# A fixed list of operations for the attention, and its 32 x 32 inverses by blocks of 16

## The chip, the core and the metric

The kernel runs on one core of a Trainium2 chip. The metric is the device time of one execution in microseconds (us). The engines are named as in the profile: PE (TensorE, with PEld for its weight loads), DVE (VectorE), ACT (ScalarE), POOL (GpSimd), SP (SyncE). SP and POOL here mostly issue DMAs.

## The reference

The program has two parts. The first is a recurrent attention with a state of 40 x 40 for each of 4 x 8 pairs of batch and head, over 768 steps of time:

```python
for t in range(S):
    ...
    y[:, :, t] = np.einsum('bhd,bhde->bhe', rt, state)
    Sa = np.einsum('bhde,bhe->bhd', state, at)
    state_decay = state * wt[:, :, None, :] - np.einsum('bhd,bhe->bhde', Sa, bt)
    state = state_decay + np.einsum('bhd,bhe->bhde', vt, kt)
```

The second is an MLP on the 3072 rows of 320 that come out: `h = x @ w_in` (320 x 2048), `g = h * tanh(softplus(h))`, `g @ w_out` (2048 x 320). Everything is float32; the MLP's weights arrive as float64.

## The kernel before

The time axis is cut into 12 chunks of 64 steps. Inside a chunk, the recurrence becomes matrix products, with one small triangular matrix per head to be inverted; from chunk to chunk, only the state is passed on. Heads are packed in two halves `be` and two pairs of partitions `al`, so most tiles have 128 partitions.

- **Preparation**, `pre_a(c, be)` (L126), 24 times. SP loads `wa` and `bk` (two buffers each); DVE makes running products of the decay by two scans (L147, L157) and scales `a` and `bk` (L152, L170); ACT spreads `a` into `ad` (L155); PE multiplies `ad` and `bk` (L186) in three groups; ACT and DVE move the result out of PSUM into `GP` (what is to be inverted) and `HA` (L188 to L193); PE transposes `bk` (L202). POOL stores `P` to DRAM. `E`, the second scan's result, lies in the half of `wa` that held `a`.
- **Inverse**, `pre_inv(n)` (L205) and `post_inv(n)` (L223), six times, each for two chunks. A chunk's 64 x 64 triangle is two diagonal 32 x 32 triangles and a square. DVE turns the triangles round (L209) so that the 128 x 32 of them lie along partitions and free rows, inverts all at once by a loop over rows, i = 1 to 30, of a multiply (L214) and an add (L216), and turns them back into `TT` (L218, and for one half `T1`, L220). PE makes the square's part by two rounds of 32 x 32 products (L232, L241); ACT lays the three pieces into `bdT` (L249 to L251); PE multiplies `HA` by it (L258) into `KT` (L260).
- **Step**, `step(c)` (L349), twelve times, with two groups `g`. POOL loads `VS`, `UVT`, `bdr` (one buffer each; L267 to L271). In each group: `step_a`, state into `VS` (L277), products with `KT` (L284), into `UVT` (L286); `step_b`, products of `UVT` and `bdr` (L314), masked into `UVQ` by DVE (L316); `step_u` and `step_d`, transposes of `UVT` and of the state (L293, L304); `step_c`, the outputs and the state's change in one PSUM tile (L334, L339), the state updated by DVE (L342, L346), the output copied to `yev` by ACT (L343) and stored by POOL (L370).
- **MLP weights**: each piece is loaded as float64 pairs (`cv_d`, L453), turned into float32 by ACT and DVE (L459 to L463) and split into a high and a low part (L494, L495). `early` does the first quarter of `w_in` at the start, `first` the other three, `second` three eighths of `w_out`, `third`, inside the MLP, the rest. All conversion buffers ahead of the MLP are single.
- **MLP**, `run` (L550): twelve blocks of 256 rows and four quarters `q`, 32 matmuls of L583 and 24 of L603 to L605 each, with Mish on ACT.

The order of the instructions on each engine comes from a scheduler outside the source. It works on single instructions, by priority; the source raises or lowers the priority of parts with `at(tc, key)` and a table `OFF` of offsets, and lays out the rough order: preparations of pair 0, inverse 0, preparations of pair 1, then for each pair the string `ORDER = '0aiA1'`: step 0 of the pair, preparations two pairs on, the inverse one pair on, weights, step 1. So matmuls of different parts can stand mixed in PE's queue. PSUM is cut into four pools of two banks.

Of the kernel before, what the change touches and what calls it, by code (L numbers as in the profile page):

```python
# [7 lines left out]
F32 = mybir.dt.float32  # L8
F32R = mybir.dt.float32r
AF = mybir.ActivationFunctionType  # L10
ALU = mybir.AluOpType
# [6 lines left out]
NA = 2  # L18
NWA = 2
NKT = 4  # L20
NXL = 1
NTT = 1
NYEV = 1
NX2 = 1
NGP = 2
NG = 2
NQ = 2
QS = "SGGG"
NU = 2
NBR = 1  # L30
NAD = 2
NTMP = 1
NP = 2
NSTN = 1
LA = 2
ORDER = '0aiA1'

OFF = {'I': 80, 'T1': 80, 'P00': -40, 'P10': 80, 'P11': 40, 'b0': 15, 'c0': 600, 'u0': -15, 'u1': 250, 'd0': 250,
       'd1': 150, 'W': 600, 'V': 400, 'E': 150, 'I0': 600, 'I1': -15, 'I2': 15, 'I3': 150, 'I4': 80, 'p4': 15,
       'I5': -150, 'J5': 600, 's0': 150, 's2': -15, 's3': 80, 's4': 250, 's6': -15, 's7': -40, 's8': 150, 's10': -150}  # L40
SORD = 'a0 b0 u0 d0 a1 b1 u1 d1 c0 c1'


def at(tc, k):
    return tc.high_priority(offset=OFF[k]) if OFF.get(k) else nullcontext()
# [33 lines left out]
def attention(ctx, tc, I, yD, pD, nch, M):  # L79
# [4 lines left out]
    ps_u = pool("ps_u", NU, space=PSUM)  # L84
    ps_q = pool("ps_q", NQ, space=PSUM)
    ps_a = pool("ps_a", NA, ictx, "right", space=PSUM)
    M.early_pools(pctx)
    ps_g = pool("ps_g", NG, pctx, "right", space=PSUM)
    cs = pool("cs", 1)
    wk = pool("wk", 2)  # L90
    ci = pool("ci", 1, ictx)
    iw = pool("iw", 2, ictx)
    cp = pool("cp", 1, pctx, "right")
    pw = pool("pw", 2, pctx, "right")
# [6 lines left out]
    wab = [cp.tile([128, 1040], F32, name=f"wa{i}") for i in range(NWA)]  # L101
    bkb = [cp.tile([128, 8, 168], F32, name=f"bk{i}") for i in range(NWA)]
    adb = [cp.tile([128, 8, 2, 2, 32], F32, name=f"ad{i}") for i in range(NAD)] * (2 // NAD)
    d1 = cp.tile([128, 584], F32, name="d1")
    bdT = [ci.tile([128, 8, 2, 64], F32, name=f"bdT{i}") for i in range(2)]
# [5 lines left out]
    for t in [d1] + [x.rearrange("p s k a t -> p (s k a t)") for x in adb[:NAD]]:  # L111
        A.copy(t, z.broadcast_to(t.shape))
    for t in bdT:
        G.memset(t, 0.0)
    VS = [cs.tile([128, 2, 344], F32, name=f"VS{be}") for be in range(2)]
    UVT = cs.tile([128, 8, 256], F32, name="UVT")
    UVQ = [cs.tile([128, 16, 104], F32, name=f"UVQ{be}") for be in range(2)]
    bdr = [cs.tile([128, 2, 8, 2, 64], F32, name=f"bdr{i}") for i in range(NBR)] * (2 // NBR)
    ST = [cs.tile([128, 8, 64], F32, name=f"ST{g}") for g in range(2)]
    for t in VS + [UVT] + bdr[:NBR] + ST:  # L120
        G.memset(t, 0.0)
# [536 lines left out]
```

## Time and profile before

| | us |
|---|---|
| median of 3 runs | 844.03 |
| lowest, highest | 843.01, 845.59 |
| span of the profiled execution | 843.5 |
| PE busy in the span | 748.6 |
| DVE busy in the span | 462.0 |
| ACT busy in the span | 429.0 |
| POOL busy in the span | 103.3 |
| mean granted TensorE clock | 0.939 |

The profile is of one execution; its span goes from the first instruction to the last. A row of the page's groups has the line, engine and operation, output and inputs by name, shapes, count, then busy time in us and the mean of one in ns, then the engine's idle time just before, and who ended it. A row of a timeline has start and length in us. Matmul ends are modelled, about 0.2 us after the work of the last one. A row of stages has, after the stage's bounds and length, the busy time of PE, PEld, DVE, ACT and POOL with counts, the granted clock, the share of the DMA engines and the DMA rate. A row of waits has the waiting engine and line, the releaser, the total in us, the number of waits and the longest. A row of one line's instructions has the least, median and greatest duration in ns and the first and last start.

### The profile page before, as it was taken

How to read it: one execution, taken by the hardware profiler on the slowest of the kernel's cores; microseconds unless marked ns; L12 is line 12 of the kernel's file. 1: busy time of each engine (PE TensorE's matmuls, PEld its weight loads, DVE VectorE, ACT ScalarE, POOL GpSimd, SP SyncE). 2: the span in 40 equal slices, each digit the busy share in tenths (PEclk: the TensorE clock that was granted, in tenths of full speed). 3: DMA queues.
4: the chain of work that ended last, by engine and by line, in shares of the span. 5: the costliest groups of instructions: out<-in, count | busy, mean ns of one | idle time of the engine just before them, and what ended most of it. 6: DMA issues, size and time to landing. Idle time of an engine off the chain costs nothing.

```text
span 843.5 us, 18796 instructions
## 1 busy us (share of the span) xinstructions
PE 748.6 (89%) x7816; PEld 695.6 (82%) x7816; DVE 462.0 (55%) x975; ACT 429.0 (51%) x937; POOL 103.3 (12%) x182
## 2 busy tenths in 40 slices
PE   2645898998989889889799899999999999999998
PEld 2534697887868778778768799999999999999998
DVE  6789879739899658788924639221222222122110
ACT  4533647774586866566738546333333333333331
POOL 8100012113122023221101200000000000000000
PEclk9855689899999999899959999999999999999999
DMA  6422223323423233323425734211120111100000
GB/s 177 134 71 64 74 63 73 90 67 105 129 81 80 66 88 103 82 67 96 123 66 142 179 109 128 54 35 36 38 54 25 31 54 35 35 21 16 16 1 32
DMA packets 58212, 61.91 MB, mean 73 GB/s; under 512 B 25536, under 2 KB 48704, under 8 KB 58128
## 3 DMA queue, kind: packets, MB, share of 16 engines
q1 hardware_dynamic: 49296, 40.94, 17.6%
q0 software_dynamic: 8832, 19.79, 9.5%
q8 instruction: 61, 1.00, 0.5%
q14 instruction: 23, 0.19, 0.1%
HBM read 48.79 MB, written 11.86 MB: 72 GB/s over the span
## 4 chain that ended last, share of the span: by engine, by line
PE 62%; DVE 15%; ACT 15%; issue 5%; DMA 2%; ACTq 0%; DVEq 0%; SPq 0%
PE ph L583 21%; PE po L604 7%; PE po L605 7%; PE po L603 7%; PE pa L186 5%; PE pa L258 4%; PE pq L314 3%; PE pq L334 2%; DVE XL L216 2%; DVE tmp L214 2%; ACT ad L155 2%; PE pu L284 1%; DMA cv_d<-in_wo 1%; DVE P L147 1%; ACT bdT L250 1%
## 5 line engine op out<-in xcount | busy, mean ns | idle before, releaser
L583 PE MATMUL ph<-xh,w_ih 128*128 128x256 f32 x576 | 148.3, 283 | 0.5 <-ACT xh L566 0.5
L585 ACT ACTIVATE g<-ph 128x512 f32<-128x512 f32 x96 | 57.3, 598 | 179.3 <-PE ph L583 179.2
L589 DVE TENSOR_TENSOR gl<-g,gh 128x1024 fp32r<-128x1024 f32 x48 | 58.7, 1225 | 160.7 <-ACT gh L588 160.4
L583 PE MATMUL ph<-xh,w_il 128*128 128x256 f32 x576 | 123.6, 283 | 0.0
L186 PE MATMUL pa<-bk,ad 128*128 128x168 f32 x384 | 85.0, 373 | 42.7 <-DVE bk L170 15.0
L604 PE MATMUL po<-w_ol,gh 128*128 128x320 f32 x384 | 118.8, 310 | 0.1
L605 PE MATMUL po<-w_oh,gl 128*128 128x320 f32 x384 | 118.4, 309 | 0.0
L603 PE MATMUL po<-w_oh,gh 128*128 128x320 f32 x384 | 117.7, 309 | 0.0
L186 PEld LDWEIGHTS pa<-bk,ad 128*128 128x128 f32 x384 | 70.8, 233 | 47.8 <-issue 22.8
L583 PEld LDWEIGHTS ph<-xh,w_ih 128*128 128x128 f32 x576 | 109.3, 190 | 0.7 <-ACT xh L566 0.7
L583 PE MATMUL ph<-xl,w_ih 128*128 128x256 f32 x384 | 101.2, 285 | 0.0
L583 PEld LDWEIGHTS ph<-xh,w_il 128*128 128x128 f32 x576 | 96.3, 190 | 0.0
L583 PEld LDWEIGHTS ph<-xl,w_ih 128*128 128x128 f32 x384 | 73.1, 190 | 0.8 <-issue 0.5
L604 PEld LDWEIGHTS po<-w_ol,gh 128*128 128x128 f32 x384 | 72.1, 188 | 0.5 <-DVE w_ol L495 0.5
L605 PEld LDWEIGHTS po<-w_oh,gl 128*128 128x128 f32 x384 | 72.1, 188 | 0.1
L603 PEld LDWEIGHTS po<-w_oh,gh 128*128 128x128 f32 x384 | 71.8, 188 | 0.0
L258 PE MATMUL pa<-bdT,HA 128*104 128x128 f32 x384 | 57.0, 304 | 9.0 <-ACT bdT L251 7.3
L258 PEld LDWEIGHTS pa<-bdT,HA 128*104 128x104 f32 x384 | 49.9, 190 | 14.4 <-ACT bdT L251 9.1
L216 DVE TENSOR_TENSOR XL<-XL,tmp 128x30 f32<-128x30 f32 (+9 forms) x180 | 59.0, 328 | 2.4
L214 DVE TENSOR_TENSOR tmp<-XL 128x30 f32<-128x30 f32 (+9 forms) x180 | 58.5, 325 | 2.5
L314 PE MATMUL pq<-bdr,UVT 128*128 128x128 f32 x384 | 57.3, 294 | 2.3 <-DVE UVQ L316 1.5
L314 PEld LDWEIGHTS pq<-bdr,UVT 128*128 128x128 f32 x384 | 50.8, 205 | 4.0 <-DVE UVQ L316 1.9
(89 smaller groups left out, 1243.5 us busy)
## 6 DMA issues: line engine op xcount, KB each, us to landing
wa<-in_wa SPq DMA_DIRECT2D x48, 162.5 KB
bk<-in_bk SPq DMA_DIRECT2D x48, 160.0 KB
cv_d<-in_wi SPq DMA_DIRECT2D x12, 512.0 KB
cv_d<-in_wo SPq DMA_DIRECT2D x8, 640.0 KB
pD<-P POOLq DMA_DIRECT2D x48, 81.2 KB, 2.2
VS<-in_vN POOLq DMA_DIRECT2D x24, 160.0 KB, 3.6
UVT<-in_vD POOLq DMA_DIRECT2D x24, 160.0 KB, 3.9
bdr<-in_rD POOLq DMA_DIRECT2D x24, 160.0 KB, 4.4
```

What stands on the lines that cost most here:

```text
L155: A.copy(ad[q, :, :, al], a[q].rearrange("p (s k t) -> p s k t", k=2, t=32))
L186: PE.matmul(pt[:, j], ad[:, s0 + j].rearrange("p k a t -> p (k a t)"), bk[:, s0 + j], start=(j == 0), stop=True, skip_group_check=True)
L214: V.tensor_tensor(out=tv, in0=X[:, i + 1:32, i:i + 1].broadcast_to([128, 31 - i, i]), in1=X[:, i:i + 1, 0:i].broadcast_to([128, 31 - i, i] ...
L216: V.tensor_tensor(out=X[:, i + 1:32, 0:i], in0=X[:, i + 1:32, 0:i], in1=tv, op=ALU.add)
L258: PE.matmul(pk[:, j], ha[:, s0 + j], bd[:, s0 + j].rearrange("p a t -> p (a t)"), start=(j == 0), stop=True, skip_group_check=True)
L314: PE.matmul(pq[:, s], UVT[:, g * 4 + s, be * 128:be * 128 + 128], br[:, be, g * 4 + s].rearrange("p a t -> p (a t)"), start=(s == 0), stop ...
L583: PE.matmul(o, w, x, start=(j == 0 and n == 0), stop=(n == 7), skip_group_check=True)
L585: A.activation(g[:, f0:f0 + 2], ph, AF.Mish)
L589: V.tensor_tensor(out=gl, in0=g, in1=gh.bitcast(F32), op=ALU.subtract)
L603: PE.matmul(po[k], gh[:, j, t], oh, start=(f == 0), stop=False, skip_group_check=True)
L604: PE.matmul(po[k], gh[:, j, t], ol, start=False, stop=False, skip_group_check=True)
L605: PE.matmul(po[k], gl[:, j, t], oh, start=False, stop=(f == 15), skip_group_check=True)
```

## The change

Nothing of the values computed changes but the way to the inverse, and nothing of the MLP's loops.

1. **A list.** Every operation of the attention and every weight conversion ahead of the MLP is first written into a list (`Plan.op`): its engine, an estimated cost, the function that issues it, what it reads and writes, a latency until others can use the result. A group of matmuls into one PSUM tile is one operation. `Plan.order` then plays the list: it takes the engine that can start first, and on it, among the operations that can start within 0.05 us of that, the one with the longest chain of work behind it. An update of the state counts 15 us more in that chain (`LATE`). Buffers of a pool are given out in that order too. The operations are issued in the order of their starts, inside `tc.manual_schedule()`. `OFF`, `at`, `SORD`, `ORDER` and the buffer constants go.
2. **The inverse by blocks of 16.** The loop runs to 14 and works on both diagonal blocks of 16 of each 32 x 32 triangle in one instruction. The block below them is the product of three: two rounds of 32 x 4 small matmuls on PE with 16 columns each, a copy by ACT between them, an add by DVE into `TT` behind them. One more transpose on DVE (`TD`) feeds the second round.
3. **Buffers.** PSUM becomes two pools of four banks, one for the steps and one for preparations and inverses; `E` gets its own tile; `stn` two buffers; `X`, `TT`, `TD`, `X2` stay single.
4. **Weights.** `early` (first quarter of `w_in`) is in the list without conditions; `first` (two quarters, two conversion buffers) can begin once all preparations are done; `second` (the last quarter and three eighths of `w_out`, two buffers) once all inverses and `first` are done. `third` and `run` are as before, behind the list.
5. **Loads of a step**: still on POOL; both loads of `UVT` now stand ahead of both of `bdr`.

The core of the diff:

```diff
+    def order(self):
+        for o in reversed(self.ops):
+            o.tail = o.cost + o.lat + max((p.tail for p in o.post), default=0.0) + o.late
...
+        while ready:
...
+            for o in ready:
+                t = max(o.ready, clock.get(o.eng, 0.0))
+                for b in o.bufs:
+                    if b.t is None:
+                        free = self.free[b.pool[0]]
+                        t = max(t, min((f for f in free if f is not None), default=1e9))
+                start[o] = t
...
+            e = min(low, key=low.get)
+            best = max((o for o in ready if o.eng == e and start[o] <= low[e] + self.look), key=lambda o: (o.tail, -o.i))
...
+            if best.mode and mode.get(e) not in (None, best.mode):
+                c += 0.13
...
+        out.sort(key=lambda o: o.start)
...
-        for i in range(1, 31):
-            tmp = iw.tile([128, 240], F32, name="tmp", bufs=NTMP)
-            tv = tmp[:, 0:(31 - i) * i].rearrange("p (t j) -> p t j", j=i)
-            V.tensor_tensor(out=tv, in0=X[:, i + 1:32, i:i + 1].broadcast_to([128, 31 - i, i]),
-                            in1=X[:, i:i + 1, 0:i].broadcast_to([128, 31 - i, i]), op=ALU.mult)
-            V.tensor_tensor(out=X[:, i + 1:32, 0:i], in0=X[:, i + 1:32, 0:i], in1=tv, op=ALU.add)
...
+        for i in range(1, 15):
+            m = 15 - i
+            tv = tmp[:, 0:2 * m * i].rearrange("p (b t j) -> p b t j", b=2, j=i)
+            ap = lambda t, j, st, sj, m=m, i=i: bass.AP(x.tensor, x.offset + 32 * t + j, [x.ap[0], [528, 2], [st, m], [sj, i]])
+            op('V', 0.16 + m * i * 0.002, lambda ap=ap, tv=tv, i=i: V.tensor_tensor(out=tv, in0=ap(i + 1, i, 32, 0), in1=ap(i, 0, 0, 1), op=ALU.mult),
+               r=['X'], w=['tmp'], lat=0.0)
...
+        op('V', 1.0, lambda: V.transpose(TD[:, :, 0:16].rearrange("p u j -> p j u"), X[:, :, 0:16].rearrange("p t j -> p j t")), r=['X'], w=['TD'])
+        X1 = X.rearrange("p t j -> p (t j)")[:, 0:512].rearrange("p (u t) -> p u t", t=16)
...
+        def m1():
+            for u in range(32):
+                for q in (slice(k * 32, k * 32 + 32) for k in range(4)):
+                    PE.matmul(zv(b1)[q, u], gp.t[q, u, 1], TT[q, u, 16:32], start=(u == 0), stop=True, skip_group_check=True)
...
+                    PE.matmul(zv(b2)[q, u], TD[q, u], X1[q, u], start=(u == 0), stop=True, skip_group_check=True)
+        op('P', 3.0, m1, r=['TT'] + allg, w=[b1], mode=32)
+        op('A', 0.54, lambda: A.copy(X1, zv(b1)), r=[b1], w=['X'])
+        op('P', 3.0, m2, r=['TD', 'X'], w=[b2], mode=32)
+        op('V', 0.62, lambda: V.tensor_tensor(out=TT[:, :, 16:32], in0=TT[:, :, 16:32], in1=zv(b2), op=ALU.add), r=[b2], w=['TT'])
...
+            op('G', 0.85, lambda q=q, al=al: G.dma_start(out=bdr[q, :, :, al].rearrange("p b s t -> p (b s) t"), in_=I['rD'][c, al]),
+               w=[('bdr', al, 0), ('bdr', al, 1)], lat=2.5)
...
+    M.early(S)
     for n in range(nds):
...
+        for c in (2 * n, 2 * n + 1):
+            for be in range(2):
+                pre_a(c, be)
+    preps = list(S.ops)
+    invs = []
+    for n in range(nds):
+        k = len(S.ops)
+        inv(n)
+        invs += S.ops[k:]
+        for c in (2 * n, 2 * n + 1):
+            step(c)
+    M.first(S, S.after(preps, lambda: (pctx.close(), M.open_first(S))))
+    M.second(S, S.after(preps + invs + S.ops[-1:], lambda: (ictx.close(), M.open_second(S))))
+    with tc.manual_schedule():
+        S.issue()
```

More of the change, by code (lines that the diff above doesn't have):

```diff
@@ L110, in attention @@
         G.memset(b, 0.0)
-    for t in [d1] + [x.rearrange("p s k a t -> p (s k a t)") for x in adb[:NAD]]:
+    for t in [d1] + [x.rearrange("p s k a t -> p (s k a t)") for x in adb]:
         A.copy(t, z.broadcast_to(t.shape))
-    for t in bdT:
-        G.memset(t, 0.0)
[L115 to L118, printed above, removed]
@@ L119, in attention @@
-    ST = [cs.tile([128, 8, 64], F32, name=f"ST{g}") for g in range(2)]
-    for t in VS + [UVT] + bdr[:NBR] + ST:
-        G.memset(t, 0.0)
+    VS = tiles(cs, 2, [128, 2, 344], "VS")
+    UVT = cs.tile([128, 8, 256], F32, name="UVT")
+    UVQ = tiles(cs, 2, [128, 16, 104], "UVQ")
+    bdr = cs.tile([128, 2, 8, 2, 64], F32, name="bdr")
+    ST = tiles(cs, 2, [128, 8, 64], "ST")
+    newBKN = make(wk, NBKN, [128, 664], "bkn")
+    newKT = make(wk, NKT, [104, 8, 128], "KT")
+    newRW = make(wk, 4, [128, 2, 16], "rw")
@@ L123, in attention @@
+    newL = S.pool("psl", 4, [ps_l.tile([128, 512], F32, name=f"pl{i}") for i in range(4)])
+    newR4 = S.pool("psr", 4, [ps_r.tile([128, 512], F32, name=f"pr{i}") for i in range(4)])
+    for t in bdT + [TD] + [UVT, bdr] + VS + ST:
+        G.memset(t, 0.0)
+    for t in S.bkn:
+        G.memset(t[:, 640:664], 0.0)
+    op = S.op
+    view = lambda b, p, n, pat, **k: b.t[p, 0:n].rearrange(pat, **k)
+    full = slice(0, 128)
     RW, W2, HA, BKN, GP, KT = {}, {}, {}, {}, {}, {}
-    LQ, SQ, OQ, PQ = (dict(S=SP, G=G, A=A)[x] for x in QS)
@@ L300, in step_d, with tr @@
             return None
[L301 to L305 removed]
+        smd, b = newSMD(), newL()
+        dv = lambda: view(b, full, 512, "p (s x) -> p s x", s=4)
+        def tr():
+            for s in range(4):
+                PE.transpose(dv()[:, s], st[:, 2 * s:2 * s + 2].rearrange("p a d -> p (a d)"), ident)
@@ L326, in step_c @@
         n = 64 if last else 104
+        bkns = [BKN[c, be] for be in range(2)]
         for s0 in range(0, 4, 2):
[L328 to L335 removed]
@@ L533, in second, with first, open_second @@
+    def first(self, S, key):
+        new = S.pool("cva", 2)
+        ops = [self.plan_in(S, new, q, k, [key]) for q in (1, 2) for k in range(3)]
+        S.after(ops, lambda: self.cvx.close())
+    def open_second(self, S):
         self.ps_h = self.pool("ps_h", NH, space=PSUM)
-        if NQ1 < 4:
-            wp = self.wp = self.pool("w2b", 1)
-            with self.tc.tile_pool(name="cvb", bufs=CVB, side="right") as cv:
-                self.w_in(wp, cv, range(NQ1, 4))
         self.mpx = self.pool("mpx", 2)
```

641 lines of the change are left out of this document (373 added, 268 removed).

## The prediction

> **What bounds the kernel now.** I read the page's busy table first, then its slices, then busy time by stage, then who waits for whom, then single instructions.
>
> ```profile
> span 843.5 us, 18796 instructions
> PE 748.6 (89%) x7816; PEld 695.6 (82%) x7816; DVE 462.0 (55%) x975; ACT 429.0 (51%) x937; POOL 103.3 (12%) x182
> PE   2645898998989889889799899999999999999998
> DVE  6789879739899658788924639221222222122110
> PEclk9855689899999999899959999999999999999999
> ```
>
> The left half of the slices is the attention, the right half the MLP, in which PE never rests. The averages of the first line mix the two. So I cut the span by events: the first stage ends where the first inverse begins (first start of L209), the second where the first chunk step begins (first start of L284), the third where the MLP stream takes over PE.
>
> ```profile
> L209 DVE STREAM_TRANSPOSE XL<-GP x6: 2090/2124/2155, 49.9 to 375.2; 128x1024 f32<-128x1024 f32 x6
> L218 DVE STREAM_TRANSPOSE TT<-XL x6: 1931/1976/2023, 97.2 to 416.2; 128x1024 f32<-128x1024 f32 x6
> L284 PE MATMUL pu<-KT,VS x768: 219/222/370, 109.7 to 484.6; 104*64 104x64 f32 x192
> ```
> ```profile
> core 0: us, PE busy (x) PEld busy (x) DVE busy (x) ACT busy (x) POOL busy (x), PEclk, DMA share, GB/s
> 0.00:49.90 49.90, 24.42 (x111) 20.93 (x112) 34.46 (x68) 25.46 (x65) 19.55 (x36) 0.86 0.51 142
> 49.90:109.70 59.80, 35.74 (x266) 30.30 (x264) 55.96 (x141) 25.99 (x72) 6.09 (x12) 0.60 0.25 73
> 109.70:484.80 375.10, 333.48 (x4686) 290.68 (x4685) 276.02 (x667) 247.03 (x610) 76.71 (x132) 0.95 0.37 94
> 484.80:843.50 358.70, 354.95 (x2759) 353.71 (x2758) 95.59 (x102) 130.56 (x190) 1.00 (x2) 1.00 0.15 42
> ```
>
> In the second stage, the first inverse, DVE is busy 56.0 of 59.8 us: DVE bounds it, and PE's clock is granted at only 0.60. In the third, PE is busy 333.5 of 375.1 us (89%) and DVE 276.0 (74%): PE is nearer its limit, with 41.6 us idle and 5% of clock withheld. The fourth is PE alone and repeats every 7.36 us:
>
> ```profile
> 549.75 3.83 PE ph L583 x32
> 557.11 3.84 PE ph L583 x32
> ```
>
> With 12 x 4 quarters that is 48 x 7.36 = 353 us, which the change does not touch. All of its effect lies ahead of 484.8.
>
> **The change part by part.**
>
> *The inverse's loop on DVE.* It falls from 30 to 14 pairs of instructions.
>
> ```profile
> L216 DVE TENSOR_TENSOR XL<-XL,tmp 128x30 f32<-128x30 f32 (+9 forms) x180 | 59.0, 328 | 2.4
> L214 DVE TENSOR_TENSOR tmp<-XL 128x30 f32<-128x30 f32 (+9 forms) x180 | 58.5, 325 | 2.5
> ```
> ```profile
> L316 DVE TENSOR_TENSOR UVQ<-pq,cst 128x512 f32<-128x512 f32 x48 | 32.9, 688 | 24.4 <-PE pq L314 24.3
> L214 DVE TENSOR_TENSOR tmp<-XL 128x108 f32<-128x108 f32 x12 | 3.2, 267 | 0.2
> L214 DVE TENSOR_TENSOR tmp<-XL 128x30 f32<-128x30 f32 x12 | 2.1, 176 | 0.2
> ```
>
> Before, 117.5 us / 6 = 19.6 us per inverse. After, both blocks of 16 go in one instruction of 2 x (15-i) x i elements, 28 to 112, together 1120. The two rows give (267 - 176) / 78 = 1.17 ns an element on 141 ns, so 14 x 0.141 + 1120 x 0.00117 = 3.3 us, twice: 6.6. Added are a second transpose of half the columns (0 to L218's 1.98; I take half, 1.0), the sum from PSUM (L316's 0.69) and a memset of 0.2. DVE does 19.6 - 6.6 - 1.9 = 11.1 us less per inverse.
>
> *Two small products on PE.* Each is 128 products of 32 x 32 by 16 columns, and a float32 matmul shows as two instructions (L241: 32 in the source, 64 in the trace), so 256 each. No row has four blocks at once on 16 columns. The nearest has two on 32:
>
> ```profile
> 102.46 1.92 PE L241 MATMUL pa<-X,GP 32*32 32x32 f32 x64 [0.79 <-ACT X L235]
> 265.30 1.20 PE L241 MATMUL pa<-X,GP 32*32 32x32 f32 x64
> ```
>
> Without the last one's tail of 0.19 that is 1.01 / 63 = 16 ns an instruction at full clock and 27 ns at the low clock of the second stage. A product then costs 256 x 16 = 4.1 us, or 6.9 cold. The lower end is 2.05, if four blocks run twice as fast as two; the upper end is the cold price. I take 4.1, the row's own. In the third stage that is ten products, +41 us of PE.
>
> [...]
>
> *The first inverse's stage.* After is in series: L209 (2.1), the loop (6.6), transpose and second transpose, two products, a copy and the sum, then what followed L218 before, 109.7 - 97.2 = 12.5 us with L218 in it. With cold products: 49.9 + 2.1 + 6.6 + 1.0 + 6.9 + 0.6 + 6.9 + 0.7 + 12.5 = 87. The four preparations of the next pair fill DVE behind it and get in the way by an instruction at a time; I add 3: step 0 begins at **90 instead of 109.7, -20 us**. Bounds: -5, if the preparations stay in front, to -27, with products at 2.05 x 27/16 = 3.5 us.
>
> *The order per engine.* Now PE's groups are not mixed: each operation issues its matmuls together. What mixing costs stands here:
>
> ```profile
> 279.02 0.55 PE L186 MATMUL pa<-bk,ad 128*128 128x168 f32 x2
> 279.50 0.24 PE L232 MATMUL pa<-TT,GP 32*32 32x32 f32 x2
> 279.68 0.55 PE L186 MATMUL pa<-bk,ad 128*128 128x168 f32 x2
> 286.79 2.05 PE L186 MATMUL pa<-bk,ad 128*128 128x168 f32 x12
> ```
>
> A round of two and two takes 279.68 - 279.02 = 0.66 us; unmixed it is 2 x (2.05 - 0.2) / 12 + 2 x 0.016 = 0.34, so a change of array shape costs 0.16. In PE's timeline of the third stage I count 239 changes in 516 groups (first and last below): 38 us. After, each of a step's six 64-column groups and each inverse's six small groups can change the shape twice, at most 12 x 12 + 5 x 12 + 20 = 224; since neighbours often share a shape, 180, so 29: **-9**. Bounds 0 to -20.
>
> ```profile
> 109.70 0.69 PE L284 MATMUL pu<-KT,VS 104*64 104x64 f32 x16
> ...
> 484.75 0.39 PE L583 MATMUL ph<-xh,w_ih 128*128 128x256 f32 x1
> ```
>
> *PE's idle time of the third stage.* Who holds PE there, and who holds ACT:
>
> ```profile
> PE pu L293 <- ACT UVT L286: 8.1, 9, 1.9
> PE pa L258 <- ACT bdT L251: 7.3, 8, 1.6
> PE pa L202 <- ACT bkn L203: 5.4, 5, 1.2
> ```
> ```profile
> ACT yev L343 <- DVE stn L342: 26.9, 20, 3.3
> DVE stn L342 <- PE pq L339: 23.2, 9, 7.7
> ```
>
> PE waits for ACT, not for DVE, though ACT is busy only 247 of 375 us. ACT in turn stands in its queue behind DVE (26.9 us), and DVE's stn behind PE (23.2). So the idle time comes from order rather than load, and a lighter DVE removes it only through those queues. A list ordered by the length of what follows, with five inverses x 11 us less on DVE, should save part: between 0 and 35 of the 41.6 I take half, **-21**.
>
> *Clock.* At 0.95 the stage loses 0.05 x 375 = 19 us. The low digits stand where PE pauses or is held; a fuller PE gets half back, **-10** (0 to -19).
>
> *Edits at nothing.* E in a buffer of its own lets the next load of wa start a little sooner; it hides behind DVE's 56 us, and without that cover costs no more than now. The loads and stores of the steps and P are the same instructions on POOL (busy 76.7 of 375) and SP. The list reckons 2.5 us for a load of bdr behind its issue; the page shows
>
> ```profile
> bdr<-in_rD POOLq DMA_DIRECT2D x24, 160.0 KB, 4.4
> ```
>
> from issue to landing, and bdr has one buffer, written after a step's last L339 and read by the next step's L314. Where the list puts L314 at its earliest, PE's queue stands behind it by about a microsecond, all later matmuls with it: 0 to +12 over twelve steps. The kernel before has the same single buffer, and its wait lies in the 41.6 already, so 0. The weight conversions get two buffers for one and lie behind the last preparations and inverses, beside the last steps' matmuls; if they come late, PE finds the first quarter of w_in ready all the same.
>
> *The seam to the MLP.* Before, MLP matmuls run ahead of 484.8 and attention matmuls after it:
>
> ```profile
> 0.00:484.80 484.80, 8.27 (x59) 7.27 (x59) 0.89 0.37 96
> 484.80:844.00 359.20, 7.72 (x128) 7.33 (x128) 2.77 (x4) 1.49 (x4) 1.00 0.15 42
> ```
>
> The first row is L583 alone, the second tile pq; 8.3 and 7.7 us cancel. After, the MLP follows the attention's whole list, and the x of chunk 0 is multiplied, cast and split in between: **+2** (0 to +6).
>
> *Sum.* Stage three: 375.1 + 41 - 9 - 21 - 10 = 376 us. Step 0 at 90, so the attention ends at 466 instead of 484.8: -19, with the seam -17. The profiled execution then spans 843.5 - 17 = 826.5; the median of the runs shown, 844.0, lies 0.5 above that span, so **827 us**.
>
> **The rivals.**
>
> *A. PE keeps its waits: slower, 858.* The waits of PE name ACT, whose work the change does not lighten (ten copies of a product more). If the list, fixed by estimated durations, queues ACT and PE no better, idle and clock stay: 375.1 + 41 - 9 = 407, end at 497, seam +2, so 843.5 + 14 = 857.5. For it speaks that PE at 89% has the new work on top and that an order frozen beforehand stalls whole queues when one duration is wrong. Against it: ACT has a third of the stage free and DVE gets another 56 us. It decides from 17 of the 31 us: if less than 14 of the idle and clock time is regained, the change is no gain. This is also the case in which the list does not do what it is said to do.
>
> *B. The small products are dear: 855.* If an instruction costs 27 ns, the row of 102.46, ten products take 69 instead of 41 us: 827 + 28 = 855. It decides at 4.1 + 17 / 10 = 5.8 us a product, 23 ns an instruction. For it: there are 256 instructions, and each carries its own weight load. Against: at full clock the row has 16 ns, and the stage has 0.95. [...]
>
> *C. Everything fits: 793.* Products at 2.05 us (-20 in the third stage), idle time down by 35 instead of 21 (-14): 793. For it: DVE then has 220 us of work in that stage, ACT 253, and preparations of the next pair can always fill PE. Against: the row for a product, and that the last steps have no preparations left to fill gaps.
>
> *D. The gain in the first inverse is not had,* since the next preparations go first as they do now: 827 + 15 = 842, no change.
>
> **How the numbers follow.** The forecast, 812 to 838 with its own bounds, gets 0.48, A 0.14, B 0.11, C 0.19, D 0.08. A measurement of this kernel cannot tell less than 0.3%, 2.5 us, from no change. Faster: nearly all of the forecast, C, a quarter of D, which makes 0.68; the same: half of D and edges of the forecast and A, 0.08; slower: the rest, 0.24. The range goes from C to A, 793 to 858: half of C and half of A lie beyond, 0.17.
>
> **What would show it.** In the profile after: L214's successor at 14 pairs and about 6.6 us per inverse, DVE 6 x 11.1 = 67 us less in all; the groups of the small products at 256 instructions in about 4.1 us each at full clock (A and B part here: 6.9 means B); the first matmul of step 0 at 90; from there to the MLP's stream about 376 us with PE's idle time near 20 and the clock near 0.97; the MLP stage unchanged at 353 us plus its ends. The prediction is wrong if the MLP's matmuls slip in between the last steps as now (some us better), if its weights come late, or if loads of bdr hold PE at every step (then L314 shows waits for that DMA).

## The result: slower by 9%, and where the profile puts it

| | before | after |
|---|---|---|
| median, us | 844.81 (4 runs) | 919.06 (4 runs) |
| lowest, highest | 843.01, 849.87 | 915.41, 922.97 |
| ratio, 95% interval | | 1.0887 [1.0829, 1.0945] |
| span of the profiled execution | 843.5 | 921.1 |
| first inverse begins | 49.9 | 46.4 |
| first step begins (`step_a`) | 109.7 | 90.4 |
| PE idle just before the MLP | none | 30.7 |

The forecast was 827 us in a range of 793 to 858. The time lies far outside, on the other side. The page of the profile after, in the lines that answer to those of before, with the row of the instruction queue and the head of the chain of work that ended last:

```profile
span 921.1 us, 24857 instructions
PE 777.9 (84%) x10888; PEld 748.4 (81%) x10888; DVE 418.7 (45%) x801; ACT 428.6 (47%) x943; POOL 102.2 (11%) x167
PE   2648888978888797969788905999999999999998
DVE  5784576439545763755451478622222222222111
PEclk9755886889599778958976966999999999999999
...
q8 instruction: 85, 1.39, 0.6%
...
PE 74%; DMA 9%; issue 5%; DVE 5%; ACT 5%; SPq 1%; DVEq 0%; ACTq 0%
```

DVE has less to do, as intended, and PE is no fuller for it: its digits in the left half are no higher than before, its clock row has 5, 6, 7 and 8 where it had 9, and a 0 stands in the slice before the MLP. The stages of after, from the first `step_a` matmul on, cut at the last attention matmul and the first MLP matmul:

```profile
90.40:531.30 440.90, 373.17 (x7393) 350.89 (x7392) 240.72 (x536) 245.55 (x634) 77.21 (x120) 0.82 0.27 72
531.30:562.00 30.70, 0.02 (x2) 0.01 (x1) 23.85 (x39) 12.75 (x19) 1.00 (x2) 0.57 0.78 248
562.00:960.00 398.00, 355.55 (x2688) 354.98 (x2688) 95.29 (x103) 133.18 (x191) 0.00 (x0) 0.99 0.13 36
```

Step 0 begins 19.3 us earlier, as was forecast, and the MLP is the same (562.0 to 921.1, 359 us). The steps' stage, 376 us by the forecast, takes 440.9: PE is busy 373.2, idle 67.7, and its clock is granted at 0.82 instead of 0.95. By the forecast PE would be busy 333.5 + 41 - 9 - 10 = 355.5 us there and idle 20.6, so 18 of the 65 us too many are busy time and 47 idle time. Behind it stands a gap of 30.7 us with no matmul. Against the forecast that is 65 + 29 us, the whole miss of 92 within 2.

Why the clock falls and PE pauses is read from PE's timeline (start and length in us, line, shape, count, idle before and who ended it) around one inverse, and from a window laid over the same place:

```profile
224.01 1.93 PE L359 MATMUL pr<-TT,GP 32*32 32x16 f32 x209
228.73 0.83 PE L359 MATMUL pr<-TT,GP 32*32 32x16 f32 x47 [2.79 <-issue]
...
231.39 1.16 PE L364 MATMUL pr<-XL,TD 32*32 32x16 f32 x72
232.71 1.90 PE L364 MATMUL pr<-XL,TD 32*32 32x16 f32 x128 [0.16 <-issue]
236.98 0.94 PE L364 MATMUL pr<-XL,TD 32*32 32x16 f32 x56 [2.38 <-issue]
...
247.65 6.08 PE L413 MATMUL pr<-bdT,HA 128*104 128x128 f32 x32 [1.68 <-ACT bdT L405]
```
```profile
229.00:252.00 23.00, 18.79 (x479) 17.27 (x472) 11.76 (x21) 11.99 (x26) 2.11 (x5) 0.50 0.27 77
```

L359 and L364 are the two small products. The first 209 matmuls of L359 run at (1.93 - 0.19) / 208 = 8.3 ns each, half of what I had taken. Then PE stands for 2.79 us and waits for nothing that the profile knows ("issue"), and finishes the 47 that are left. L364 has the same pause. From there to 252 the clock is granted at 0.50, for 23 us, though PE is busy 18.8 of them; it comes back beside the dense L413. Who holds PE in the steps' stage, and who holds DVE and SP's queue:

```profile
PE pr L359 <- issue: 15.1, 6, 3.3
PE pr L306 <- ACT HA L313: 11.9, 8, 2.7
PE pr L364 <- issue: 10.4, 6, 2.4
```
```profile
DVE bk L277 <- DMA bk<-in_bk: 57.5, 18, 5.7
```
```profile
SPq L663 <- PE pr L329: 61.5, 1, 61.5
```

So there were three suspects: the small products, by their pauses and the low clock behind them; the seam, where the first load of the remaining weights stood in SP's queue for 61.5 us behind the last preparation's transposes (L329); and loads of `bk` that come later than the list reckons. Against all three stood the view that the list's frozen order loses the time, whatever the inverse does. Where an expectation below names one of them by a letter, F is the products, S the seam and L the list.

### The profile page after: what moved, and what is told of

It reads as the page before. It is cut to its first block, busy times and chain, and to the rows that moved or that the text cites. A ratio compares the mean times of both kernels' runs of the same rounds, so it can differ in the third digit from the quotient of the medians.

```text
span 921.1 us, 24857 instructions
## 1 busy us (share of the span) xinstructions
PE 777.9 (84%) x10888; PEld 748.4 (81%) x10888; DVE 418.7 (45%) x801; ACT 428.6 (47%) x943; POOL 102.2 (11%) x167
## 4 chain that ended last, share of the span: by engine, by line
PE 74%; DMA 9%; issue 5%; DVE 5%; ACT 5%; SPq 1%; DVEq 0%; ACTq 0%
PE ph L771 20%; PE po L792 6%; PE po L793 6%; PE po L791 6%; PE pr L413 6%; DMA bk<-in_bk 5%; PE pl L489 4%; PE pr L306 4%; PE pl L517 4%; PE pr L364 3%; PE pr L329 3%; DMA wa<-in_wa 2%; DMA cv_d<-in_wi 2%; PE pl L462 2%; PE pl L449 2%
## 5 line engine op out<-in xcount | busy, mean ns | idle before, releaser
L771 PE MATMUL ph<-xh,w_ih 128*128 128x256 f32 x576 | 149.6, 285 | 30.8 <-ACT xh L754 30.7
L306 PE MATMUL pr<-bk,ad 128*128 128x168 f32 x384 | 86.6, 393 | 38.8 <-DVE bk L277 19.1
L306 PEld LDWEIGHTS pr<-bk,ad 128*128 128x128 f32 x384 | 77.5, 253 | 43.3 <-issue 24.7
L413 PE MATMUL pr<-bdT,HA 128*104 128x128 f32 x384 | 59.5, 325 | 12.1 <-ACT bdT L405 10.0
L413 PEld LDWEIGHTS pr<-bdT,HA 128*104 128x104 f32 x384 | 56.0, 212 | 15.2 <-ACT bdT L405 11.7
L277 DVE TENSOR_TENSOR bk<-bk,E 128x1024 f32<-128x1024 f32 x24 | 29.2, 1218 | 59.8 <-DMA bk<-in_bk 59.8
L776 ACT CAST gh<-g 128x1024 fp32r<-128x1024 f32 x48 | 50.3, 1048 | 1.2
L329 PE MATMUL pr<-cst,bk 128*128 128x128 f32 x192 | 38.4, 352 | 12.4 <-ACT HA L313 8.7
L489 PE MATMUL pl<-bdr,UVT 128*128 128x128 f32 x384 | 45.7, 277 | 0.6 <-ACT UVT L452 0.6
## 6 DMA issues: line engine op xcount, KB each, us to landing
cv_d<-in_wi SPq DMA_DIRECT2D x12, 512.0 KB
```

Of the source, the lines that this page charges most:

```text
L306: PE.matmul(pv()[:, j], ad[:, s0 + j].rearrange("p k a t -> p (k a t)"), bk[:, s0 + j], start=(j == 0), stop=True, skip_group_check=True)
L329: PE.transpose(pv()[:, j].rearrange("p a b -> p (a b)"), bk[:, s0 + j, xo:xo + 128], ident)
L413: PE.matmul(kv()[:, j], ha.t[:, s0 + j], bd[:, o + s0 + j].rearrange("p a t -> p (a t)"), start=(j == 0), stop=True, skip_group_check=True)
L489: PE.matmul(qv()[:, s], UVT[:, g * 4 + s, be * 128:be * 128 + 128], bdr[:, be, g * 4 + s].rearrange("p a t -> p (a t)"), start=(s == 0), s ...
L771: PE.matmul(o, w, x, start=(j == 0 and n == 0), stop=(n == 7), skip_group_check=True)
L776: A.copy(gh, g)
```

## The experiments

All times are in us. On the chips that ran them, the kernel before took 845.34 (one run, e1 to e4), 841.46 (one run, e5 to e8), 845.79 (median of 17, e9 to e12) and 843.80 (median of 11, e13 and e14). Runs of one kernel spread by 8 to 12 us (before, on one chip: 835.69 to 848.10), so smaller differences are not read from single runs. Every edit of the list or of its costs also changes the order that the list chooses for all else; e13 will show that this alone can be worth more than 15 us.

### e1: the weights early (S)

The choice of the list gets a bonus for the last two chunks' transposes and their sums of decay, so that what the weights wait for is done sooner.

```diff
-            best = max((o for o in ready if o.eng == e and start[o] <= low[e] + self.look), key=lambda o: (o.tail, -o.i))
+            best = max((o for o in ready if o.eng == e and start[o] <= low[e] + self.look), key=lambda o: (o.tail + o.boost, -o.i))
...
-            op('P', 0.45, tr, r=BK + ['cst'], w=[b], mode=128, claim=[bkn])
+            op('P', 0.45, tr, r=BK + ['cst'], w=[b], mode=128, claim=[bkn], boost=300.0 * (c >= nch - 2))
```

> Edit: in the list, the transposes of the last pair of preparations and their small sum get a bonus in the choice of the next operation, so that nothing but they moves ahead and the weights' first loads may begin earlier. Theory S (PE stands still between attention and MLP because the loads of w_in wait for the last preparation's transposes, issued last): the gap on PE of 30.7 us before the first MLP matmul falls to 12 or less, the attention from step 0 (90 us) to its last matmul stays at 441 +- 6, the span comes to 893 to 905. Rival (x of chunk 0 or the conversions' work on DVE and ACT sets the gap whenever they begin, or they slow the last steps): gap over 22 or attention longer by as much, span over 912.

Measured: 900.8. The stages:

```profile
88.90:536.00 447.10, 376.94 (x7393) 356.43 (x7392) 251.48 (x553) 250.09 (x640) 77.33 (x120) 0.81 0.29 78
536.00:540.20 4.20, 0.03 (x1) 0.03 (x1) 4.00 (x7) 3.32 (x8) 1.01 (x2) 1.00 0.76 190
```

The gap falls from 30.7 to 4.2, the stage grows by 6 and keeps its clock of 0.81. S is shown, as expected, and is worth about 20 us (18 in the time, 22 in the span); it has nothing to do with the clock of the steps' stage.

### e2: the list with the old loop (F against L)

The loop of 30 rows goes back into the list, and the products out of it.

```diff
-        for i in range(1, 15):
...
+        for i in range(1, 31):
+            tv = tmp[:, 0:(31 - i) * i].rearrange("p (t j) -> p t j", j=i)
...
-        op('P', 3.0, m1, r=['TT'] + allg, w=[b1], mode=32)
...
-        op('P', 3.0, m2, r=['TD', 'X'], w=[b2], mode=32)
```

> Edit: the list stays, the inverse goes back to the loop of 30 rows on DVE, with no small products on PE. Theory F (the products' 512 instructions in a row outrun the fetch of PE's instructions; the pauses and the thin work around them bring the granted clock down to 0.5 for some 20 us in each inverse): from step 0 to the attention's last matmul the mean clock is 0.92 or more instead of 0.82, the stage lasts 385 to 400 instead of 441, step 0 begins at about 100 instead of 90, the gap before the MLP stays near 30, the span is 870 to 885. Rival O (the list's order itself leaves PE idle and cold, whatever the inverse): clock 0.86 or less, stage 425 or more, span 910 or more.

Measured: 895.55. The stage, and PE's first wait in it:

```profile
89.50:518.60 429.10, 334.56 (x4769) 311.96 (x4768) 298.43 (x696) 250.72 (x643) 77.67 (x120) 0.85 0.30 81
```
```profile
PE pr L360 <- DVE TT L347: 34.2, 4, 8.6
```

PE's work is that of before (334.6 against 333.5) and no product pauses, yet the stage takes 429 us: PE now waits for DVE's loop (34.2 us in that row), and its clock is low too, at 0.85. In clock and stage it came out as rival O has it, in the span (893.4) between the two. So F alone does not explain the loss; the list has a share that doesn't come from the products, in the clock too: of the stage's clock 0.15 x 429.1 = 64 us are withheld, against 79 in after and 19 before. Step 0 begins at 89.5, with the loop of 30 rows.

### e3: dense matmuls inside the products (F: pause or clock)

Eight matmuls of 128 x 128 x 512, whose output nobody reads, are laid between the small ones of each product. Their cost in the list goes from 3 to 9 us with it.

```diff
+                if u % 4 == 3:
+                    PE.matmul(b3.t, ident, tmx, start=True, stop=True, skip_group_check=True)
```

> Edit: in each small product, after every 16 small matmuls one full 128 x 128 by 512 matmul whose result nobody reads (eight a product, some 7 us of full-clock work, so 70 us in ten products). Theory F: the fetch keeps up (no pause inside a product) and PE's clock stays up, mean 0.92 or more from step 0 on; what the clock gives back (about 40 us) and the pauses (about 25) pay for most of the added work, so the stage is 430 to 455. Rival O: the clock stays at 0.82 to 0.86 and the stage grows by 45 or more, to 485 and above.

Measured: 949.11.

```profile
101.50:585.50 484.00, 435.80 (x7536) 351.35 (x7535) 248.41 (x550) 250.24 (x640) 77.52 (x120) 0.92 0.27 72
```

PE is busy 62.6 us more in the stage (435.8 - 373.2) and idle 19.5 less (48.2 instead of 67.7), and the stage is 43.1 longer, 1 us short of rival O's bound. The clock is that of F: it rises from 0.82 to 0.92, and no wait inside the products is under issue any more. So with dense work between the small matmuls both the pauses and most of the low clock go. What the higher clock is worth in time can't be read apart here, since it lies inside the 62.6, and the added matmuls cost more than they bring.

### e4: half the products (F)

`range(32)` becomes `range(16)` in both products, so half of the block below the diagonal is not computed.

> Edit: each small product is made for 16 of the 32 blocks along its free axis (256 instructions instead of 512), the other 16 are left out, so their part of the inverse is missing. [...] Rival G (the clock falls because the 32-row work and the chain of the inverse leave PE too thin, pauses or not): the pauses go, but the clock stays at 0.84 or less and the stage falls by little more than the 20 us of pauses and halved work, to 418 to 430. Rival O: stage 430 or more.

Measured: 885.49, and in the page 73 blocks of instructions where after has 85:

```profile
82.50:493.60 411.10, 352.27 (x6113) 331.17 (x6112) 239.45 (x536) 243.56 (x634) 77.05 (x120) 0.85 0.29 77
```

```profile
PE pr L364 <- issue: 3.9, 3, 1.8
PE pr L359 <- issue: 1.1, 2, 0.6
```
```profile
218.40:235.40 17.00, 15.30 (x299) 14.33 (x287) 13.03 (x23) 11.50 (x27) 3.06 (x6) 0.50 0.38 112
```

The stage loses 30 us: PE is busy 20.9 less and idle 8.9 less. The pauses inside the products fall from 25.5 us in 12 to 5.1 in 5, but other waits of PE take the place of more than half of that. And the clock hardly follows the pauses. At 0.85 it lies just above the 0.84 of rival G, and the last row shows why: half the clock for 17 us, from 218.4 on, beside an inverse whose products have no pause at all. PE's longest wait in the 10 us ahead of 218.4 is 1.16 us, for ACT's copy between the two products. The trace has such a stretch of 17.1 us behind each of the five inverses of the stage. It has the same five in e2, which has no small products, and in after one of 17.1 and four of 23.9. So the larger part of these stretches comes with the thin work and the waits that an inverse leaves to PE in the list's order, and the pauses lengthen them.

### e5: the loads' durations

The list's costs and latencies for SP's and POOL's loads are set to what the profile shows of them.

```diff
-            op('S', 0.1, lambda q=q, al=al: SP.dma_start(out=bk[q, :, xo:xo + 128], in_=I['bk'][c, be, al]), w=[('bk', be, al)], lat=2.5)
+            op('S', 0.8, lambda q=q, al=al: SP.dma_start(out=bk[q, :, xo:xo + 128], in_=I['bk'][c, be, al]), w=[('bk', be, al)], lat=4.5)
```

`wa` gets 0.4 and 3.5, `UVT` and `bdr` latencies of 3.1 and 3.5.

> Edit: only costs in the list, set to what the profile shows: issue of a wa load 0.4 and of a bk load 0.8 us on SP instead of 0.1, latency 3.5 and 4.5 instead of 2.5, of UVT 3.1 and of bdr 3.5 instead of 2.5. Theory D (DVE's queue is held in 18 places, 57 us, by a bk that the list reckons to be there, and what stands behind it holds PE): DVE's waits for bk fall under 20 us, the stage from step 0 to the attention's last matmul falls from 441 to 415 to 428, the span to 895 to 908 with the gap before the MLP still near 30. Rival B (bk's buffer comes free late, so the load is late however it is listed): the waits stay over 40 us or turn up at another place, the stage stays at 436 to 446, the span at 915 or more.

Measured: 904.71.

```profile
91.30:529.00 437.70, 375.68 (x7397) 350.02 (x7396) 243.70 (x548) 249.47 (x644) 76.90 (x120) 0.82 0.30 78
529.00:543.90 14.90, 0.00 (x0) 0.00 (x0) 10.41 (x16) 6.15 (x10) 1.01 (x2) 0.58 0.88 266
```

DVE's wait for `bk` falls from 57.5 to 8.6, but the stage is only 3 us shorter, as rival B has it: DVE then waits for PE (`HA` at L314 for L306: 30.5 instead of 8.9). The gain of 14 is in the gap, since the new order puts the weights earlier. The earlier loads alone hardly shorten this stage.

### e6 and e14: the block inverse in the kernel before (F against L)

e6 puts the inverse by blocks, line for line, into the kernel before, under its own scheduler. e14 is e6 with the priority of the two products raised, so that each stands in PE's queue in one stretch; in e6 the twelve of them stood in 99 stretches.

```diff
+        with tc.high_priority(offset=2000):
             for u in range(32):
                 for q in (slice(k * 32, k * 32 + 32) for k in range(4)):
                     PE.matmul(z1[q, u], gp[q, u, 1], TT[q, u, 16:32], start=(u == 0), stop=True, skip_group_check=True)
```

> Edit: the kernel before with its own scheduler and priorities, and only the inverse by blocks of 16 with its two small products a pair put in. Theory L (most of the loss comes from the fixed list, not from the inverse): the MLP's stream starts at most 8 us later than before (484.8), the granted clock from step 0 on is 0.93 or more, the time 832 to 852. Theory F (the products, with fetch pauses and cold clock behind them, carry the loss): pauses of 2 to 3 us inside the products as in the changed kernel, 15 us or more in all, the clock from step 0 on at 0.90 or less, the time 860 to 885.

> As e6 (the block inverse in the kernel before, 935.5 us), with each of the products raised in priority so that its 128 matmuls stand together in PE's queue; in e6 they stood in 99 stretches. Nothing is left out. If e6 lost by the mixing (shape changes and short stretches of a low clock): near the kernel before, 845 to 875 us. If whole products lose by pauses of 2 to 3 us and the low clock behind them whatever order surrounds them, as in after: 895 to 925 us, with the clock of the stage at 0.82 to 0.87. If both orders are equally bad: 930 us or more.

Measured: 935.51 and 915.97. The stages, first of e6, then of e14, and then PE's first waits in e14's:

```profile
91.70:583.30 491.60, 419.47 (x7435) 364.87 (x7435) 250.68 (x559) 262.07 (x647) 77.64 (x134) 0.86 0.30 77
```
```profile
93.20:564.70 471.50, 407.75 (x7442) 360.94 (x7442) 248.13 (x559) 261.03 (x646) 77.86 (x134) 0.85 0.31 80
```
```profile
PE pa L235 <- issue: 10.3, 7, 2.1
PE pa L229 <- issue: 9.7, 4, 3.5
```

Without any list, the inverse by blocks alone costs the kernel before 94 us in e6 and 72 in e14. For e6 that is far more than either theory expected, for e14 it is the second case. L is refuted as the only cause. Whole products bring the same pauses under issue (20.0 us at L229 and L235) and a clock of 0.85 in an order that has nothing to do with the list. The 20 us between the two runs may be the price of mixing: counted over PE's timeline, e6 has 370 changes of shape in the stage and e14 280 (before 239), and at the 0.16 us of the prediction those 90 would be 14 of the 20.

### e7: the products in eight pieces (F)

Each product becomes eight operations of 32 matmuls (16 in the source), which the list may set no closer than 1 us apart; a product costs 2.4 us in it instead of 3.0. The instructions and the bytes stay the same, and the list finds another order for all of them.

```diff
-        def m1():
-            for u in range(32):
+        def m1(p):
+            for u in range(4 * p, 4 * p + 4):
...
-        op('P', 3.0, m1, r=['TT'] + allg, w=[b1], mode=32)
+        for p in range(8):
+            op('P', 0.30, lambda p=p: m1(p), r=['TT', (b1, p - 1)] + allg, w=[(b1, p)], mode=32, lat=1.0)
```

> Edit: in the list, each small product is eight operations of 64 instructions, each of which may begin 1 us after the end of the one before, so that the list puts other matmuls between. Theory F: no pause over 1 us inside a product, the clock from step 0 on rises from 0.82 to 0.86 or more, the stage falls from 441 to 410 to 428; step 0 begins up to 15 us later (90 to 105), since nothing else is there to fill the first inverse. Rival G (the clock falls because the inverse's chain leaves PE with thin work, pauses or not): pauses go, the clock stays at 0.83 or less, the stage at 432 or more.

Measured: 877.59.

```profile
105.80:501.20 395.40, 347.48 (x7325) 318.04 (x7324) 225.02 (x501) 237.24 (x602) 75.62 (x116) 0.90 0.29 81
```

```profile
PE pr L364 <- issue: 2.6, 1, 2.6
```

The stage falls from 440.9 to 395.4, below what F expected, and the clock rises from 0.82 to 0.90. PE is busy 26 us less with the same matmuls but 68, which run ahead of the stage. The pauses in the products fall from 25.5 us in 12 to this one (all of PE's waits under issue from 28.0 to 6.4; an expectation below counts 27.6 in after), though the changes of shape rise from 113 to 208. So the same instructions cost much in a burst and little when they are spread. How much of the gain is the pauses and how much the dense work that now stands between the pieces, as in e3, this run can't say.

### e8 to e10: the three mends together

e8 and e10 are one kernel: e1, e5 and e7 at once. e9 has e1 and e5 on e2, so the old loop in a mended list.

> The list of after with the loop of 30 rows (no products, as in e2), the weights' first load ahead of the last transposes (as in e1) and the loads' durations of e5. It asks what the block inverse is worth once the list's other two faults are mended: e8 with blocks in pieces took 840.8 us, e2 with the loop 895.6. Theory (the block inverse does take DVE off the path, and only its instruction pauses and the cold clock took that gain away): the gap of 15 us before the MLP goes and the rows of bk come earlier, but DVE's loop keeps 65 us in stage 3, so 860 to 880 us, clock 0.85 to 0.9. Rival (the products bring nothing, the list's order was all): 835 to 850 us. Rival (the loop's DVE waits are the bound of the list whatever the loads do): 880 us or more.

> The kernel of e8 once more, timed against the kernel before. Theory: with the products in pieces, the weights early and the loads' durations set, the list gives what it lost, and no more: 836 to 846 us, a ratio of 0.99 to 1.003. Rival (e8 was a lucky single run): 850 us or more. Rival (it beats the kernel before by over 0.5 per cent): below 838 us.

e8 took 840.77 in one run; from the gains of the three edits one by one I had expected a span of 855 to 885, and it was 839.0. Timed several times beside the kernel before: e9 878.63, ratio 1.0378 [1.0311, 1.0445]; e10 840.26, ratio 0.9930 [0.9891, 0.9968]. The stages of e9 and of e10, and PE's first wait in e10's:

```profile
83.00:500.60 417.60, 327.43 (x4853) 307.96 (x4852) 303.49 (x710) 247.75 (x645) 79.42 (x124) 0.87 0.31 82
```
```profile
95.70:479.10 383.40, 339.96 (x7331) 314.26 (x7331) 231.97 (x519) 241.37 (x609) 74.10 (x114) 0.93 0.34 89
```
```profile
PE pr L364 <- issue: 7.6, 2, 6.0
```

Both came out as their theories expected. With the mends the change is no longer slower: 79 us are back, and e10 takes 0.7% less than the kernel before, which is too little to call it faster. Between e9 and e10 only the inverse differs in the source, and the second is 38 us shorter, more than the changes of order in e11 and e13: the lighter DVE is a gain, once the products don't stop PE.

### e11, e12, e13: what is needed of it

e12 is e10 without the loads' durations. e11 has 16 pieces 0.6 us apart in place of 8. e13 leaves the first inverse's products whole, at 2.4 us each in the list.

> As e8 without the loads' durations: products in pieces and the weights early, wa and bk planned as in after. e7 with pieces alone took 877.6 us with a gap of 15.4 us before the MLP. If the load's lateness costs its own time, the gap goes and the rest stays: 858 to 868 us, and DVE's wait for bk in stage 3 is above 30 us. If e8's gain over e7 came from the seam alone: 838 to 848 us.

> As e8, with each product in 16 pieces of 32 instructions, 0.6 us apart in the list, instead of 8 of 64. If only the bursts of instructions matter, 8 pieces already take the pauses away (6.9 us of 27.6 left) and 16 give the same within 5 us: 836 to 846 us. If the pauses that are left still cost the clock, 16 pieces raise it over 0.92 and give 825 to 836 us. If each change of shape costs what the mixing cost in e6, up to 160 changes more at 0.16 us add 10 to 25 us: 850 to 866 us.

> As e10, but the first inverse's two products stay whole, since no steps stand beside them to fill the gaps between pieces. With pieces, step 0 began at 95.7 us in e10 and at 116.9 in e11 with its 16 pieces; with whole products at 90.4 in after. If the pieces only delay the first inverse there, step 0 begins near 90 and the time is 832 to 838 us. If nothing follows from it because the later stage takes the time back: 839 to 844 us. If two whole products cost the clock of the first steps: 845 us or more.

Measured: e12 869.16, ratio 1.0274 [1.0197, 1.0351]; e11 854.89, 1.0111 [1.0040, 1.0183]; e13 856.67, 1.0168 [1.0117, 1.0219]. DVE's wait for `bk` in e12 and in e10, then two stages of e11 and one of e13:

```profile
DVE bk L277 <- DMA bk<-in_bk: 33.4, 9, 7.4
```
```profile
DVE bk L277 <- DMA bk<-in_bk: 10.3, 4, 4.7
```
```profile
41.70:116.90 75.20, 52.05 (x874) 43.99 (x874) 57.78 (x140) 30.16 (x85) 6.09 (x12) 0.59 0.25 70
116.90:499.80 382.90, 353.07 (x7236) 316.06 (x7236) 223.06 (x490) 238.66 (x601) 73.98 (x114) 0.93 0.33 89
```
```profile
98.10:499.70 401.60, 352.79 (x7315) 324.86 (x7315) 245.52 (x548) 249.55 (x634) 77.39 (x120) 0.91 0.33 88
```

e12: the loads' durations, worth 14 us in after, are worth 29 once the products are in pieces, 9 of them ahead of step 0 (104.5 in e12, 95.7 in e10). That the products had hidden the late loads before is an inference. e11: its steps take 382.9 us, as in e10, with PE busy 13 us more and idle 14 less; nearly all of its loss lies ahead of step 0, at 116.9 instead of 95.7. The time lies in the range of my third expectation, but by luck: none of the three had the loss there. e13: whole products did not bring step 0 forward (98.1), so the pieces were not what delayed it in e10, and the stage behind, with the same operations from the second inverse on, came out 18 us longer. Most of that lies between step 0 and step 2, which take 76.1 us instead of 60.4. The list now begins the second inverse at 112.0 instead of 90.7, and step 2 needs it; PE is idle 11.8 us there instead of 5.1, and its clock is 0.91 instead of 0.97. From step 2 on the two take 325.5 and 323.0. I expected 832 to 838 and was wrong. The time is that of my third case, but the low clock stands behind the second inverse, from 147.6 on, and not behind the whole products. Why the list chooses the later inverse stays open.

## Why the prediction was wrong, point by point

**Right, one part of it by luck.** Step 0 at 90: it begins at 90.4. But I put these 20 us down to the shorter loop, and the list brings as much with the old one. From the first inverse to step 0 it is 59.8 us before, 44.0 in after, 44.4 in e2 (the list with the loop of 30 rows) and 43.8 in e6 (the blocks without the list). Either change alone is enough, and they do not add.

The loop at 6.6 us an inverse, and the added DVE work, were right:

```profile
L348 DVE TENSOR_TENSOR XL<-XL,tmp 128x28 f32<-128x28 f32 (+6 forms) x84 | 20.4, 242 | 2.4
L346 DVE TENSOR_TENSOR tmp<-XL 128x28 f32<-128x28 f32 (+6 forms) x84 | 19.9, 237 | 2.3
...
L351 DVE STREAM_TRANSPOSE TD<-XL 128x512 f32<-128x512 f32 x6 | 6.7, 1110 | 0.0
...
L368 DVE TENSOR_TENSOR TT<-TT,pr 128x512 f32<-128x512 f32 x6 | 4.1, 689 | 37.4 <-PE pr L364 37.4
...
L340 DVE MEMSET XL<- 128x256 f32 x6 | 1.6, 272 | 0.7
```

(20.4 + 19.9) / 6 = 6.7. By rows DVE does 117.5 - 40.3 - 6.7 - 4.1 - 1.6 = 64.8 us less, against 67. The MLP unchanged, and no wait of `step_b` for `bdr`: right. Changes of shape are fewer still than forecast, 113 in the stage instead of 180, which at the prediction's price would be 126 x 0.16 = -20 and not -9. No run shows that price alone; in e11, with 345 changes against e10's 220, PE is busy 13 us more, an estimated 0.10 us a change.

**A size that was off.** DVE's busy time fell by 43.3 us, not 67. Rows of DVE overlap, and I had added them up. In the kernel before, DVE's timeline has

```profile
381.30 0.33 DVE L216 TENSOR_TENSOR XL<-XL,tmp 128x168 f32<-128x168 f32 x1
381.57 0.43 DVE L461 TENSOR_SCALAR cv_w<-cv_m 128x512 int32<-128x512 int32 x1
381.92 0.34 DVE L214 TENSOR_TENSOR tmp<-XL 128x184 f32<-128x184 f32 x1
```

L461 starts at 381.57, before L216 ends at 381.63, and L214 before L461 ends. So an instruction between two of the loop cost less here than its row. Over the span, the lengths of all of DVE's instructions add up to 512.0 us before and 449.3 after, its busy time to 462.0 and 418.7: the sum fell by 62.7, and 19.4 of that was overlap. What the loop's going frees is therefore less than its rows' sum.

**The step that failed first: the price of a product.** I took 4.1 us between 2.05 and 6.9, from 16 ns an instruction. The instruction itself was dearer in that estimate than in fact: 8.3 ns at full clock, 2.1 us a product, the lower bound. What I left out is that 256 matmuls and 256 weight loads in one burst are not done in that time. From 224.01 to the end of its last piece at 229.56 the product took 5.55 us, the next one, 231.39 to 237.92, 6.53; the ten of the stage took 60 us instead of 41, though PE was busy in them for only 34.6 (14.6 at L359, 20.0 at L364). So rival B had the price, above its own line of 5.8 us, and not the reason.

The pauses fit the page's row of instructions: PE's 10888 matmuls and 10888 loads over 85 blocks are 256 instructions a block, as in the kernel before (15632 over 61). The trace's records of these blocks show them, in the burst, starting 4.0 to 4.3 us apart (221.5, 225.6, 229.8, 233.8), while a product at 8.3 ns a pair uses up two blocks in 2.1 us. No two blocks of the run start closer than 3.3 us. And the records tell when the pauses end: each of the 15 waits of PE under issue longer than 0.9 us ends 1.2 to 1.9 us after the record of a block ends (226.88 for the pause that ends at 228.73, 235.44 for that of 236.98). The same holds for the pauses in the products of e14, under the other scheduler (1.2 to 1.5 us). e4 (half the instructions, a fifth of the pauses) and e7 (the same instructions, spread, a tenth) show that the burst is what counts. That PE waits there for its instructions is what these records say together; no run changes the blocks' arrival by itself.

**The step that failed most: the clock.** I expected a fuller PE to get half of the lost clock back, -10 us. PE got no fuller, and the clock went from 0.95 to 0.82: 0.18 x 440.9 = 79 us of the stage's clock withheld, against 19 before. That is not all lost time, since PE also waits in these stretches (4.2 of the 23 us from 229 to 252), but PE's busy time came out 18 us above the forecast although the products took 6 less of it. In the trace 113 of the stage's 155 us at half clock stand behind the five inverses, and the other 42 are about what the kernel before has in all (41). I had looked at how full PE is on average, and the clock fell where an inverse leaves PE with small products, transposes and waits, one inverse after the other. The products' pauses are a part of that and no more: e4 has a fifth of the pauses and still 0.15 x 411.1 = 62 us withheld, e2 has no small products and 64. What lifted the clock was dense work between the small matmuls: in e3 (0.92 instead of 0.82), and in pieces in e7 (0.10 x 395.4 = 40 us) and e10 (0.07 x 383.4 = 27). How the loss divides between the list's order and the products is open, since e2 and e14 each show most of it alone. The clock's records of before and after hold 1 and 0.5 and nothing between. In after a pause of 2.8 us, and in e4 waits of at most 1.16, had half the clock behind them, and in after it stayed at half over 23 us with PE busy 18.8 of them. By what rule it falls and comes back was not shown.

**The idle time** was to fall from 41.6 to 20.6 and rose to 67.7: 25.5 us of it are the pauses, and PE's other long waits name ACT, as before, now for `HA` and `bdT`. In e10 it is 383.4 - 340.0 = 43.4, that of before. So the list brings none of the 21 us that I credited it with, even when mended. Rival A, that an order frozen by estimated durations queues no better, was right in this and in its sign, and too mild in its price, since it kept idle time and clock where they were.

**The seam** was +2, with the words that late conversions do no harm because the first quarter of `w_in` is there. It was +30.7. SP's and PE's timelines:

```profile
513.73 19.77 SPq L663 DMA_DIRECT2D cv_d<-in_wi  x6
...
544.41 0.33 SPq L626 DMA_DIRECT2D xy<-yD  x1
```
```profile
512.99 0.66 PE L329 MATMUL pr<-cst,bk 128*128 128x128 f32 x4
...
561.99 1.01 PE L771 MATMUL ph<-xh,w_ih 128*128 128x256 f32 x3 [30.68 <-ACT xh L754]
```

The quarter was there, but the MLP's input was not: its load (L626) stood in SP's queue behind the loads of the weights, its sum (L753, 560.12) in DVE's queue among their conversions, and its cast (L754, 561.11) waited for that sum. I had asked whether PE's weights would be late and not what else was queued behind the late load. e1 shows the place and the price.

**A cause I had as nothing at all**: DVE's wait for `bk` (57.5 us). The list reckoned an issue of SP at 0.1 us and a landing at 2.5. I looked at such a latency for `bdr`, where it did no harm, and not for the loads on SP. Alone its mending took 14 us off, all but 3 of them in the seam, and with the products in pieces 29.

Together: from 919.1, pieces take off 41.5 (e7), the weights then 8.4 (e12), the loads then 28.9 (e10); what is left of the whole change is then a gain of 0.7%. The 8.4 are no more than the spread of single runs, and each step also holds the list's new order, for which e11 and e13 show some 15 us. What stays open: how the 41.5 divides between pause and clock, how the 72 us of e14 do, and why the list chose worse orders in e11 and e13 than in e10.

## What to carry to other kernels

Price a group of very small matmuls by the instructions it puts into the queue, not by their rows: count them, divide by the rate at which blocks of instructions start in the trace (in after's burst 256 instructions in 4.0 to 4.3 us), and if a burst outruns that, spread it between dense matmuls (e7's stage took 395.4 us instead of 440.9). Ask not only how full PE is on average but where it is thin, since in after and e4 each of the five inverses of the stage had half the clock for 17 to 24 us, with long pauses or without. And where an order is frozen from estimated durations, look first at the ones that are cheapest in the estimate, and ask of a late transfer what else is queued behind it.

## What the runs showed of the hardware that was not expected

- Four blocks of 32 x 32 by 16 columns, side by side, run at 8.3 ns an instruction at full clock and 13.5 at half ((1.90 - 0.19) / 127 at 232.71), against the 16 and 27 that the prediction took from blocks in pairs. A whole product of after's stage still took 6.0 us, by its pauses and not by the distance of its matmuls.
- At 224.01 PE took 209 small matmuls with their loads without a break, and then none for 2.79 us, until 1.85 us after the record of the next block of instructions had ended. The 85 blocks of after, 256 instructions each, start at least 3.3 us apart, an estimated 26 ns for a matmul with its load (3.29 / 128).
- Half clock lasted 23 us in after with PE 82% busy (229 to 252), and 17 us in e4 with PE 90% busy; in after it ended beside a group of dense matmuls, the 32 of L413 at 247.65.
